# One normalising operation per four heads, with attention rows of 640 floats and their heads interleaved

## The chip, the core and the metric

The kernel runs on one core of one Trainium2 chip. A core has TensorE (PE; its weight loads are listed apart as PEld), VectorE (DVE), ScalarE (ACT), GpSimd (POOL) and SyncE (SP), which issues DMA transfers. The engines run side by side, each works through its own instructions in order, and they wait for one another with semaphores. The metric is the device time of one execution in microseconds (us); the median of the runs is compared.

## The reference

Attention over eight batches and eight heads of 576 queries, against keys and values pooled by eight to 72, followed by a mixture of experts: each token goes to the expert with the largest of eight logits, and its output is scaled by the gate's probability and by a second, sigmoid gate.

```python
k_p = k.reshape(B, H, Sp, pool, D).mean(axis=3)        # B=8, H=8, S=576, D=64, pool=8
v_p = v.reshape(B, H, Sp, pool, D).mean(axis=3)
attn = softmax(scale * q @ k_p.T)
x = (attn @ v_p).transpose(0, 2, 1, 3).reshape(B * S, H * D)      # 4608 x 512
logits = x @ w_gate                                    # 8 experts
e_idx = argmax(logits, axis=1)
eom = 1 / (1 + exp(-(x @ w_output_gate)))
for e in range(E):
    h = maximum(x[mask] @ w1[e], 0.0)                  # 512 -> 1024
    ye = h @ w2[e]                                     # 1024 -> 512
    out[mask] = gate_w[mask, None] * eom[mask, e, None] * ye
```

## The kernel before

**Attention and routing** work through 36 tiles of 128 tokens. Each tile has two halves (`a` is 0 or 1) of four heads, and a loop (L531 to L561) interleaves the steps of several tiles by hand. For half `a` of tile `i`:

- `scores` (L228): TensorE multiplies queries with the pooled keys; `peak` (L234): VectorE takes each head's maximum; `softmax` (L239): ScalarE exponentiates; `transpose_p` (L248, L249) turns the result two tiles later.
- `values` (L256): three tiles later TensorE multiplies the turned weights with `vbd`, the pooled values, into a PSUM tile `av`, of which there are two. Each head has COLS = 81 columns there: 64 outputs, 16 columns with that head's part of the two gates' logits, and the softmax's sum. L273 takes the sums' reciprocals on VectorE.
- `normalise` (L279, L281): VectorE multiplies the outputs by the reciprocals into `xg`, the tile's row of 512 floats in the order head, feature. A second operation does the same with the 4 x 16 logit parts, into a tile `graw` in the order head, logit.

For every group of four tiles `route` (L291 to L357) adds the eight heads' logit parts (L296), finds the expert and the token's place in that expert's list, and writes the gate's factor into the row. It is a chain of small VectorE operations that `work` spreads between the steps of the tiles. A row in `xg` has ROW = 514 floats: 512 features, the token's number (written by an `iota` on POOL, L268) and the factor (L344). POOL scatters each tile's rows to a table `xs` in device memory, by an indirect DMA per tile (L390), sorted by expert.

Beside this run the loading of keys, queries, values and the first weights (SP), the pooling of keys and values (POOL at L173, L174 and L188, VectorE at L191), and the splitting of the first weights in a high and a low part (L416 on ScalarE, L420 on VectorE).

**The change of stages.** `gather_early` (L395) waits for the rows of the first six groups and gathers the first three tiles of expert 0 into `xb` with three indirect DMAs. `turn_x` (L427 to L430) transposes each in four slices of 128 features, as the first layer wants them. Then the first layer's first job runs (L581) while `route` of the last group and `closing` (L361) compute the table of jobs on VectorE.

**The experts** take jobs of two or three tiles of 128 rows. For each, TensorE transposes the gathered rows (L830), multiplies with `w1` (L868) and with `w2` (L849); every factor is split in a high and a low part. ScalarE and VectorE move and split the results, VectorE applies the factor (L999), and POOL gathers the rows of a later job (L1085) and scatters the outputs (L1110). The weights of the even experts lie in `w1a` and `w2a`, those of the odd ones in `w1b` and `w2b`; SP loads pieces of them into six `stage` buffers.

**Memory.** The buffer `rows` holds `xb`, then the outputs `y_all`, then some scratch for the list of tiles (`past_rows` in the place of `y_all`, `line_rows` behind it). `w1b` and `w2b` are allocated behind `rows`.

## Time and profile before

| | |
|---|---|
| median of three runs | 664.21 us (663.7 to 667.07) |
| the profiled execution | 664.95 us, of which the span is 663.2 us |
| granted clock of TensorE, mean of the span | 0.98 |
| attention ends (last L281 starts) | at 180.0 us |
| first L849 of the experts' stage starts | at 199.68 us |
| DVE busy, of the span | 356.3 us (54%) |
| PE busy, of the span | 612.9 us (92%) |

All times inside the execution are counted from the start of the span. The shares of the span mix the two stages, so the stages have to be read apart. The profile names an instruction by its line, its engine, its operation, and the tiles that it writes and reads (`xg<-av,grec`); `x72` is how often it ran. A group's line gives the busy time of all and the mean of one. Two VectorE instructions in a row can overlap in the profile: the next one starts before the last one ends.

### The profile page before, as it was taken

Reading aid. Unit: us, or ns where it says so; the run is one execution under the profiler, and the core shown is the slowest. Engines: PE = TensorE matmul, PEld = TensorE weight load, DVE = VectorE, ACT = ScalarE, POOL = GpSimd, SP = SyncE. Lnnn points to the kernel's source line nnn. Section 1 sums busy time; section 2 is a strip of 40 time slices with the busy share of each in tenths; the row PEclk is TensorE's granted clock in tenths of the full one; section 3 lists DMA queues with packets and bytes.
Section 4 is the critical chain, followed back from the end, with each engine's and each line's share of the span. In section 5 each row is a group of like instructions: output and inputs, shape, how many; then the busy total and the mean of one; then the engine's idle time right before and its main releaser. Section 6 shows DMA issues by size and latency. Waiting matters only on the chain.

```text
span 663.2 us, 11977 instructions
## 1 busy us (share of the span) xinstructions
PE 612.9 (92%) x3715; PEld 558.4 (84%) x3716; DVE 356.3 (54%) x877; ACT 260.0 (39%) x693; POOL 217.4 (33%) x270
## 2 busy tenths in 40 slices
PE   0898988999978999999999999999998899999996
PEld 0787877988976999899798988999897898989895
DVE  5689989899883722577546422354142722222221
ACT  2776857888541511347244301333040420211110
POOL 3547628663432321231404112131222213030213
PEclk9998988999998899999989999999999899999999
DMA  8899757883435921467746422074113102020203
GB/s 268 275 290 285 225 181 263 251 231 121 129 144 177 315 80 49 122 215 248 272 139 209 149 70 61 19 231 134 55 22 134 32 20 80 16 63 32 64 32 77
DMA packets 28746, 95.82 MB, mean 144 GB/s; under 512 B 4735, under 2 KB 5759, under 8 KB 26882
## 3 DMA queue, kind: packets, MB, share of 16 engines
q1 hardware_dynamic: 18194, 61.92, 29.5%
q0 software_dynamic: 10480, 33.13, 15.1%
q8 instruction: 21, 0.34, 0.2%
q14 instruction: 51, 0.42, 0.2%
HBM read 76.13 MB, written 20.22 MB: 145 GB/s over the span
## 4 chain that ended last, share of the span: by engine, by line
PE 66%; issue 2%; DVE 1%; DVEq 0%; POOL 0%; ACT 0%; POOLq 0%
PE p_y L849 32%; PE p_h L868 31%; PE p_x L830 2%; DVE w1a L993 1%; PE p_y L830 0%; POOL out L1110 0%; DVE rows L999 0%; DVE xt L986 0%; ACT xt L933 0%; PE p_y L910 0%; DVE sums L1019 0%; DVEq L681 0%; DVEq L1018 0%; DVEq L1030 0%; DVEq L798 0%
## 5 line engine op out<-in xcount | busy, mean ns | idle before, releaser
L948 ACT ACTIVATE ht<-p_h 128x384 fp32r<-128x384 f32 (+1 forms) x104 | 46.8, 450 | 267.0 <-PE p_h L868 266.7
L868 PE MATMUL p_h<-xt,w1b 128*128 128x384 f32 (+1 forms) x736 | 117.8, 321 | 4.1 <-issue 3.0
L868 PEld LDWEIGHTS p_h<-xt,w1b 128*128 128x128 f32 x736 | 116.6, 191 | 5.4 <-issue 3.5
L849 PE MATMUL p_y<-w2a,ht 128*128 128x512 f32 x456 | 109.1, 399 | 6.2 <-issue 4.2
L1006 DVE SCALAR_TENSOR_TENSOR ht<-p_h,ht 128x384 fp32r<-128x384 f32 (+1 forms) x104 | 52.5, 505 | 114.9 <-ACT ht L948 114.8
L849 PE MATMUL p_y<-w2b,ht 128*128 128x512 f32 x480 | 113.6, 396 | 0.0
L849 PEld LDWEIGHTS p_y<-w2a,ht 128*128 128x128 f32 x456 | 87.1, 193 | 25.0 <-issue 6.7
L849 PEld LDWEIGHTS p_y<-w2b,ht 128*128 128x128 f32 x480 | 89.8, 188 | 20.5
L868 PE MATMUL p_h<-xt,w1a 128*128 128x256 f32 (+1 forms) x640 | 95.1, 309 | 4.2 <-DVE sums L1019 4.2
L868 PEld LDWEIGHTS p_h<-xt,w1a 128*128 128x128 f32 x640 | 94.4, 193 | 5.0 <-DVE sums L1019 4.4
L999 DVE TENSOR_SCALAR rows<-p_y,sc 128x512 f32<-128x512 f32 x41 | 30.5, 749 | 122.7 <-PE p_y L849 122.7
L1110 POOL DMA_INDIRECT out<-rows,dst x41 | 41.6, 1015 | 129.7 <-DVE rows L999 124.9
L256 PE MATMUL av<-vbd,pT 128*128 128x162 f32 (+1 forms) x480 | 75.6, 313 | 8.5 <-DVE vbd L216 2.9
L239 ACT ACTIVATE p<-p_h,m 128x72 f32<-128x72 f32 x288 | 70.9, 361 | 25.4 <-DVE m L234 25.2
L256 PEld LDWEIGHTS av<-vbd,pT 128*128 128x128 f32 (+1 forms) x480 | 62.8, 185 | 11.9 <-issue 6.4
L1085 POOL DMA_INDIRECT rows<-xs,src x51 | 58.6, 1149 | 24.2 <-POOL src L1081 13.9
L1080 POOL COPY nx<-rows 128x6 f32<-128x6 f32 x17 | 3.2, 190 | 149.1 <-PE p_y L830 71.2
L390 POOL DMA_INDIRECT xs<-xg,where x36 | 36.0, 1000 | 47.2 <-DVE where L345 22.9
L228 PE MATMUL p_h<-kbd,q_even 128*128 128x144 f32 (+1 forms) x160 | 30.6, 321 | 15.7 <-DMA q_even<-qT 12.2
L249 ACT ACTIVATE pT<-ptr 128x384 f32<-128x384 f32 x72 | 37.8, 526 | 5.7 <-PE ptr L248 5.6
L228 PEld LDWEIGHTS p_h<-kbd,q_even 128*128 128x128 f32 (+1 forms) x160 | 24.5, 203 | 17.1 <-issue 12.2
L248 PE MATMUL ptr<-ident,p 128*128 128x128 f32 x216 | 37.2, 283 | 1.8 <-DVE running L333 1.7
(172 smaller groups left out, 712.2 us busy)
## 6 DMA issues: line engine op xcount, KB each, us to landing
stage<-wst SPq DMA_DIRECT2D x64, 512.0 KB, 5.3
kq<-kT SPq DMA_DIRECT2D x7, 1152.0 KB
rows<-v SPq DMA_DIRECT2D x16, 288.0 KB
kq<-qT SPq DMA_DIRECT2D x4, 1152.0 KB
q_even<-qT SPq DMA_DIRECT2D x3, 1152.0 KB
rows<-v SPq DMA_DIRECT2D x8, 256.0 KB
rows<-v SPq DMA_DIRECT2D x8, 160.0 KB
kq<-kT SPq DMA_DIRECT2D x2, 576.0 KB
```

Of the source, the lines that this page charges most:

```text
L228: nc.tensor.matmul(s[r0:r0 + n, 144 * c:144 * c + 144], q_t[b][:, 2 * a + c, s0:s0 + n], kbd[b % 2][:, 2 * a + c, :], start=True, stop=True)
L239: nc.scalar.activation(pt[i % 3][:, 4 * a + h, 0:KEYS], sv[:, h], AF.Exp, bias=m[:, h:h + 1])
L248: nc.tensor.transpose(tr[:, P * c:P * c + P], src[:, o:o + P], ident)
L249: nc.scalar.activation(pT_t[i][:, 3 * a:3 * a + 3, :], tr[:, 0:384].rearrange("p (c n) -> p c n", c=3), AF.Copy)
L256: nc.tensor.matmul(av[r0:r0 + n, COLS * c:COLS * c + 2 * COLS], pT[:, 3 * a + c, r0:r0 + n], vbd[b % 2][:, a, c].rearrange("p h f -> p (h ...
L390: ins = nc.gpsimd.indirect_dma_start(out=xs, out_offset=bass.IndirectOffsetOnAxis(ap=where, axis=0), in_=x.bitcast(I32), in_offset=None)
L849: i = mm(p_y[k], ht[:, h, f, P * k:P * k + P], w[:, part, o:o + DM], start=(f == 0 and part == 0 and h == 0), stop=(f == 7 and h == 1))
L868: i = mm(to, w[:, part, o:o + P], x, start=(d == 0 and k == 0), stop=(d == 3 and k == len(terms) - 1))
L948: act(ht[:, 0, f, 0:size * P], p_h[f % 3][:, 0:size * P], AF.Relu).then_inc(q["hh"], 1)
L1006: nc.vector.scalar_tensor_tensor(ht[:, 1, f, 0:n], src, 0.0, ht[:, 0, f, 0:n].bitcast(F32), op0=ALU.max, op1=ALU.subtract).then_inc(q["hl" ...
L1085: nc.gpsimd.indirect_dma_start(out=xb[:, k].bitcast(I32), out_offset=None, in_=xs, in_offset=bass.IndirectOffsetOnAxis(ap=src[:, k:k + 1], ...
L1110: nc.gpsimd.indirect_dma_start(out=out, out_offset=bass.IndirectOffsetOnAxis(ap=dst[:, k:k + 1], axis=0), in_=yb[k], in_offset=None, bound ...
```

## The change

A row of `xg` gets 642 floats. Each half tile has HALF = 4 x (64 + 16) = 320 of them, in the order feature, head: the four heads' values of one feature lie side by side, and behind the 256 features follow the 64 logit parts in the same order (logit, head). The token's number and the factor are the last two floats (ID = 640).

`normalise` is one VectorE operation per half tile in place of two. It reads 80 columns of each head, in the order head, column, and writes `xg` with four floats between one column and the next. `graw` goes. `route` sums the logit parts straight out of `xg`, over the halves and the heads.

Everything that reads the rows follows: `features` gives the four slices of 128 features for the transposes; the rows of `w1` are brought into the same order on the host; the number and the factor are read at ID. The indirect DMAs move 642 floats per row. In `rows`, `line_rows` now lies in the space of `y_all`, behind `past_rows`; the buffer grows by 160 floats in each partition, and what is allocated behind it, `w1b` and `w2b` among it, moves by 640 bytes.

```diff
-ROW = DM + 2
+
+HALF = 4 * (D + 16)
+ID = 2 * HALF
+ROW = ID + 2
...
+def features(x, c):
+    o = HALF * (c // 2) + P * (c % 2)
+    return x[:, o:o + P]
...
-        nc.vector.memset(zrow[:, DM:DM + 1], float(N))
+        nc.vector.memset(zrow[:, ID:ID + 1], float(N))
...
-                graw[g] = p2.tile([P, GMAX, H, 16], F32, tag="graw", name=f"graw{g}")
...
-                nc.gpsimd.iota(xg[g][:, 0:n, DM], pattern=[[P, n]], base=t0 * P, channel_multiplier=1,
+                nc.gpsimd.iota(xg[g][:, 0:n, ID], pattern=[[P, n]], base=t0 * P, channel_multiplier=1,
...
-        nc.vector.tensor_tensor(xg[g][:, j, D * 4 * a:D * 4 * a + 4 * D].rearrange("p (h d) -> p h d", h=4), avv[:, :, 0:D],
-                                grec[g][:, j, hs].unsqueeze(2).to_broadcast([P, 4, D]), op=ALU.mult)
-        nc.vector.tensor_tensor(graw[g][:, j, hs], avv[:, :, D:D + 16], grec[g][:, j, hs].unsqueeze(2).to_broadcast([P, 4, 16]),
-                                op=ALU.mult)
+        nc.vector.tensor_tensor(xg[g][:, j, HALF * a:HALF * a + HALF].rearrange("p (f h) -> p h f", h=4), avv[:, :, 0:D + 16],
+                                grec[g][:, j, hs].unsqueeze(2).to_broadcast([P, 4, D + 16]), op=ALU.mult)
...
-        gw = graw[g][:, 0:n]
+        gw = xg[g][:, 0:n, 0:ID].rearrange("p j (a f h) -> p j f a h", a=2, h=4)[:, :, D:D + 16]
         lg = small(g, [P, n, 16], F32, "lg")
-        v_.tensor_reduce(lg, gw.rearrange("p j h f -> p j f h"), axis=AX.X, op=ALU.add)
+        v_.tensor_reduce(lg, gw, axis=AX.XY, op=ALU.add)
...
-        v_.reciprocal(xg[g][:, 0:n, DM + 1], rec)
+        v_.reciprocal(xg[g][:, 0:n, ID + 1], rec)
...
-            nc.tensor.transpose(tr[:, c], sh.xb[:, k, P * c:P * c + P], ident)
+            nc.tensor.transpose(tr[:, c], features(sh.xb[:, k], c), ident)
...
 def line_rows(sh, c0, c1):
-    o = WIDE * (ROW + DM) + 112
+    o = WIDE * ROW + 2 * (E - 1) * R
...
-                i = nc.tensor.transpose(p_x[k][:, c], xb[:, k, P * c:P * c + P], sh.ident)
+                i = nc.tensor.transpose(p_x[k][:, c], features(xb[:, k], c), sh.ident)
...
-            copy(nx, xb[:, :, DM:DM + 2]).then_inc(q["c"], 1)
+            copy(nx, xb[:, :, ID:ID + 2]).then_inc(q["c"], 1)
...
-        sh.rows = sb("rows", [P, WIDE * (ROW + DM) + 112 + 2 * R + 26], F32)
+        sh.rows = sb("rows", [P, WIDE * (ROW + DM) + 26], F32)
...
-            moe_w1.reshape(E, 4, P, FF).transpose(0, 2, 1, 3).reshape(E, P, 4096),
+            moe_w1.reshape(E, 2, 4, D, FF).transpose(0, 1, 3, 2, 4).reshape(E, 4, P, FF).transpose(0, 2, 1, 3).reshape(E, P, 4096),
```

More of the change, by code (lines that the diff above doesn't have):

```diff
@@ L218, in gate_v @@
                                     mask.unsqueeze(3).to_broadcast([P, 3, 2, 16]), op=ALU.mult)
-    s_t, pT_t, xg, graw, grec = {}, {}, {}, {}, {}
+    s_t, pT_t, xg, grec = {}, {}, {}, {}
     GMAX = max(GROUPS)
```

## The prediction

> **What bounds the kernel now.** I read the page first, then the busy time by stretches, the groups by line and form, the waits of TensorE, and the order of time in single stretches.
>
> ```profile
> PE 612.9 (92%) x3715; PEld 558.4 (84%) x3716; DVE 356.3 (54%) x877; ACT 260.0 (39%) x693; POOL 217.4 (33%) x270
> ```
>
> This is the page's line of busy time (engine, us, share, instructions). The stretches below give, after the bounds and the length, the busy time of PE, PEld, DVE, ACT and POOL, then PE's granted clock, the DMA share and GB/s:
>
> ```profile
> 40.00:60.00 20.00, 16.41 (x121) 14.51 (x120) 18.82 (x55) 13.04 (x51) 10.16 (x7) 0.91 0.98 295
> 60.00:80.00 20.00, 19.90 (x164) 18.82 (x164) 18.65 (x69) 16.14 (x63) 13.96 (x13) 1.00 0.76 235
> 80.00:100.00 20.00, 17.02 (x130) 15.54 (x130) 17.14 (x58) 13.24 (x51) 8.19 (x5) 0.91 0.59 216
> 100.00:120.00 20.00, 17.64 (x132) 15.94 (x131) 19.66 (x62) 13.99 (x53) 16.66 (x14) 0.91 0.77 257
> 120.00:140.00 20.00, 18.88 (x161) 17.47 (x159) 17.81 (x68) 15.67 (x60) 13.56 (x12) 1.00 0.82 256
> 140.00:160.00 20.00, 18.99 (x156) 17.46 (x153) 19.55 (x81) 17.92 (x70) 7.78 (x7) 1.00 0.49 148
> 160.00:180.00 20.00, 18.88 (x155) 17.63 (x154) 16.95 (x76) 14.34 (x48) 7.97 (x9) 1.00 0.39 140
> ...
> 340.00:380.00 40.00, 40.00 (x234) 37.15 (x233) 23.05 (x32) 17.35 (x28) 9.31 (x14) 1.00 0.60 194
> ```
>
> The page's 54% for DVE is an average over two stages with different limits. In the experts' stage TensorE alone sets the pace: from 340 to 380 us PE is busy 40.00 of 40.00. Attention, before it, has two engines near full: from 40 to 180 us the seven rows add up to 127.7 of 140 for PE and 128.6 for DVE. DVE has 11.4 us free there, PE 12.3. In four stretches of 20 us (40, 60, 100 and 140) DVE has only 1.18, 1.35, 0.34 and 0.45 us free. The next view, TensorE's waits in 40 to 184 us (total, times, longest), says who ends PE's idle time; its five longest:
>
> ```profile
> PE av L256 <- DVE vbd L216: 2.9, 1, 2.9
> PE av L256 <- DVE grec__3_1365 L339: 1.9, 1, 1.9
> PE ptr L248 <- DVE running L333: 1.7, 1, 1.7
> PE av L256 <- DVE graw L281: 1.6, 2, 1.1
> PE av L256 <- DVE zr L316: 1.5, 2, 1.1
> ```
>
> All name DVE: 9.6 us of PE's idle time. So work added to or taken from DVE in attention is felt in the span, though not one for one.
>
> **The change, part by part.** *One normalisation instead of two.* First the groups by form (us of all, mean ns of one), then a piece of DVE's order of time (start and length in us):
>
> ```profile
> L279 DVE TENSOR_TENSOR xg<-av,grec 128x256 f32<-128x256 f32 x72 | 30.3, 421 | 1.2
> ...
> L191 DVE TENSOR_REDUCE vp<-rows 128x64 f32<-128x256 f32 x42 | 23.9, 596 | 2.6 <-POOL rows L188 2.6
> ...
> L281 DVE TENSOR_TENSOR graw<-av,grec 128x64 f32<-128x64 f32 x72 | 15.3, 213 | 0.0
> ...
> L296 DVE TENSOR_REDUCE lg<-graw 128x64 f32<-128x512 f32 x9 | 9.2, 1024 | 0.0
> ...
> L191 DVE TENSOR_REDUCE vp<-rows 128x192 f32<-128x1536 f32 x2 | 5.5, 2756 | 4.9 <-DMA rows<-v 4.9
> ...
> L316 DVE TENSOR_REDUCE zr<-zs 128x4 f32<-128x32 f32 x9 | 1.6, 177 | 0.1
> ```
>
> ```profile
> 60.78 0.42 DVE L279 TENSOR_TENSOR xg<-av,grec 128x256 f32<-128x256 f32 x1
> 61.12 0.21 DVE L281 TENSOR_TENSOR graw<-av,grec 128x64 f32<-128x64 f32 x1
> 61.25 0.45 DVE L234 TENSOR_REDUCE m<-p_h 128x4 f32<-128x288 f32 x1
> ```
>
> The pair shows 421 + 213 ns, but successive operations overlap: start to start L279 takes 0.34 us and L281 0.13, so the pair holds DVE for 0.47 us. From 64 to 256 elements the time grows by 208 ns in 192, 1.083 ns an element. With dense writes the one operation of 320 elements would hold DVE for 0.34 + 64 x 1.083 ns = 0.41 us: 0.06 us saved, not the 0.21 of a whole operation.
>
> Its writes are not dense. The input runs through 80 adjacent floats of a head, and the output places them four floats apart, since the four heads are interleaved: each write lies 16 bytes behind the last. No row of this trace has a long strided write. The nearest rows are strided reads of SBUF: L191 sums values 64 floats apart, and between its two forms 1280 elements cost 2160 ns, 1.69 ns each, 0.60 above the dense rate. Bounds for the write: no excess (0.41 us), 0.60 as for the reads (0.41 + 320 x 0.60 ns = 0.60 us), or twice that (0.80 us). I take the middle, the only strided price that a row shows: +0.13 us x 72 = **+9.5 us of DVE**.
>
> The Trainium skill has this price ("Vector Engine (DVE) Microarchitecture Reference", 5.2 Measured stream behaviour on trn2): a port keeps its full rate only where elements come in runs of two or more adjacent 4-byte words, and the destination counts like the sources. The page gives 1.71 ns for a destination that hops at every element, about the reads' 1.69 above, and 2.50 for one that steps by 24 words; by the latter the operation would hold DVE some 0.86 us and the sum on DVE would be some +25 us, an estimate from that page. No row here shows a write.
>
> *The logits' sum.* L296 now reads floats 16 apart: 1024 ns for 512, the strided rate. Afterwards four neighbours lie together and the halves 320 floats apart. At the dense rate, from L316's 177 ns for 32 elements, it takes 177 + 480 x 1.083 = 697 ns: 0.33 x 9 = **-2.9 us**. If runs of four don't help, 0.
>
> DVE's net is +6.6 us, and the first row below (shortest, median and longest, first and last start) spreads the 72 calls over 154 us: 0.86 in each 20 us. In the four full stretches I let nine tenths through to PE (3.1), in the other three, with 2.2 to 3.1 us free, a third (0.9): **+4.0 us**. All of it would be 6.6, a third 2.2.
>
> ```profile
> L279 DVE TENSOR_TENSOR xg<-av,grec x72: 409/424/426, 26.0 to 179.7; 128x256 f32<-128x256 f32 x72
> ...
> L331 DVE TENSOR_SCALAR gden<-gden x9: 157/170/3989, 54.0 to 183.0; 128x4 f32<-128x4 f32 x9
> ```
>
> ```profile
> 106.09 3.58 POOL L188 TENSOR_TENSOR rows<-rows 128x768 f32<-128x768 f32 x2
> ...
> 105.72 3.99 DVE L331 TENSOR_SCALAR gden<-gden 128x4 f32<-128x4 f32 x1
> ```
>
> A second reason to expect less than all: small DVE operations are held up beside POOL's long ones. L331, 170 ns in the median, once took 3989 and ended with POOL's L188. DVE that comes later to such a place ends at the same moment; shifted, it can also meet or miss one. That is worth 3 us either way, and I keep it for the range.
>
> *Longer rows.* The 36 scatters and 54 gathers move 642 floats a row instead of 514, a quarter more. The DMA view (times, us to landing) and the order of time have:
>
> ```profile
> rows<-xs,src POOLq DMA_INDIRECT x54, 4.2
> ...
> xs<-xg,where POOLq DMA_INDIRECT x36, 4.9
> ```
>
> ```profile
> 169.08 1.12 POOL L400 DMA_INDIRECT rows<-xs,src  x1 [0.30 <-issue]
> ...
> 173.06 0.63 ACT L416 ACTIVATE w1a<-stage 128x512 fp32r<-128x512 f32 x1
> ...
> 174.54 0.63 PE L427 MATMUL xtr<-ident,rows 128*128 128x128 f32 x4 [1.12 <-ACT w1a L416]
> ...
> 199.98 1.05 POOL L1085 DMA_INDIRECT rows<-xs,src  x1 [0.83 <-POOL src L1081]
> ...
> 193.95 2.35 DVE L420 TENSOR_TENSOR w2a<-stage,w2a 128x1024 fp32r<-128x1024 f32 x2
> ```
>
> and from the chain that ended last:
>
> ```profile
> 212.33 0.45 PE p_x L830 x4
> ```
>
> One transfer counts: the second early gather (issued 169.08). PE waits 1.12 us for it until 174.54; ACT's L416, which the row names, ended at 173.69, so the gather is the likelier releaser. A row set of 263 KB at the 140 to 295 GB/s of the stretches above takes 0.9 to 1.9 us, 1.2 at some 220, so a quarter more is **+0.3 us**; bounds 0 and 1 (a quarter of a landing). In the experts' stage a gather has time: issued at 199.98, its first reader on PE is at 212.33, against 4.2 us to land. Without that cover the 17 later sets of three gathers would cost 0.3 each, 5 us. DMA issues on POOL and SP keep their number and order.
>
> *The end of attention.* DVE runs almost without a gap from the last normalisation to its last part of w2a (193.95, 2.35 us), so the last L296's -0.33 and the last normalisation's +0.13 act there directly: **-0.2 us**.
>
> *At nothing:* the weight rows' new order (same loads and matmuls); the transposes' slices, still 128 adjacent floats; the zero row's memset, 128 floats on one partition, in the start stretch. Moving w1b and w2b by 640 bytes:
>
> ```profile
> L868 PE MATMUL p_h<-xt,w1b 128*128 128x384 f32 x480 | 85.3, 338 | 0.0
> ...
> L868 PE MATMUL p_h<-xt,w1a 128*128 128x384 f32 x288 | 50.5, 334 | 0.0
> ```
>
> The two w1 buffers lie at different addresses and differ by 4 ns in 334, so I take 0 and keep 1 us either way.
>
> **Sum:** 4.0 + 0.3 - 0.2 = +4.1 us. The profiled execution took 664.95 us (span 663.2); with 4.1 it is 669.05. The median of the runs shown is 664.21, 0.74 below it, and 664.21 + 4.1 gives **668.3 us**.
>
> **The rivals.** *Writes at 16 bytes are free (the other side).* Place: the 72 calls; price: 0.41 us instead of 0.47, so -4.4 - 2.9 = -7.3 us on DVE. It decides if an excess of under 0.2 ns an element is paid (0.06 us over 320). About half passes, since only the 9.6 us of PE's waits on DVE can shrink and a held-up operation doesn't end sooner: -3.6, with +0.3 and -0.4 at the end -3.7: 660.5 us. [...] Against it: the reads' 1.69 ns. The Trainium skill ("SBUF — State Buffer", Door 1) says that SBUF lines have 16 bytes, and that fp32 can be strided by 4 for free, but also that two hits a line are needed; the second, with one hit a line here, speaks against it. No row here settles it.
>
> *Short hops cost double.* At 0.80 us the change adds 0.33 x 72 = 23.5, less 2.9: +20.6, of which 140/154, 18.7, between 40 and 180 us. DVE then has 128.6 + 18.7 = 147.3 us of work for 140. Of its 11.4 us free, 7.4 are waits for av, by its row in DVE's waits of 40 to 184 us; the other 4.0 lie between instructions and stay. 147.3 + 4.0 - 140 = +11.3, with +0.1 from the rest: 675.6 us. The 2.50 ns of the Trainium skill's page above would land here.
>
> ```profile
> DVE grec L273 <- PE av L256: 7.4, 11, 1.5
> ```
>
> *It is swallowed.* DVE's 11.4 us free take all of it, and only the +0.1 from transfer and end is left: 664.3 us. Against it: DVE ends PE's waits in every full stretch.
>
> **How the numbers follow.** A measurement of this kernel can tell about 0.5%, 3.3 us, from no change: under 660.9 is faster, over 667.5 slower. Forecast 0.62 (own range 665.5 to 671.5, from a third to all of 6.6 us), free writes 0.13, double 0.20, swallowed 0.05. Faster: half of the free writes and a little chance, 0.08. Same: the other half, the swallowed case and a quarter of the forecast, 0.28. Slower: 0.64. The range 664.0 to 676.5 leaves out the free writes and the top of the double case.
>
> **What would show it.** The one normalisation's mean: near 685 ns (421 + 64 x 1.083 + 320 x 0.60) for the forecast, 490 for free writes, near 880 for double. The logits' sum near 700 ns. DVE's busy time in attention up by about 6 us, PE's waits on DVE longer, and the experts' stage as long as before. I am wrong if the mean is 490, or if it is 685 and attention still ends where it did.

## The result and the profile after

| | before | after |
|---|---|---|
| median, same chip | 664.92 us (663.7 to 667.07, 4 runs) | 656.78 us (654.11 to 661.12, 4 runs) |
| ratio, 95% interval | | 0.9872 [0.983, 0.9914] |
| profiled execution (span) | 664.95 us (663.2) | 657.38 us (655.7) |
| granted clock of TensorE, mean | 0.980 | 0.987 |
| first L849 / L854 of the experts' stage | 199.68 us | 196.47 us |

The kernel became faster by 1.3%, where 668.3 us, slower by 0.6%, was forecast. One run of one kernel below (the changed kernel with the move taken back, 667.7 us) fell in a slower state of the chip and is left out of that kernel's figures. The lines of the new kernel lie 7 or 8 further down in attention (L279 is L286, L216 is L224) and 5 further in routing and experts' stage (L296 is L301, L849 is L854, L868 is L873).

First the groups by line and form of the kernel after (us of all, mean ns of one, idle time before), which answer to the rows of the prediction:

```profile
L286 DVE TENSOR_TENSOR xg<-av,grec 128x320 f32<-128x320 f32 x72 | 53.5, 743 | 1.2
...
L301 DVE TENSOR_REDUCE lg<-xg 128x64 f32<-128x512 f32 x9 | 6.0, 667 | 0.0
```

The one normalisation takes 743 ns (685 forecast), and start to start it holds VectorE for 0.584 us in the median (0.60 forecast; the pair before 0.472): 0.112 x 72 = 8.0 us more. The logits' sum fell by 357 ns x 9 = 3.2 us (2.9 forecast). VectorE has 4.8 us more to do, in place of the 6.6 forecast. So the price of the strided writes was read well; and yet the time fell.

Now TensorE's waits of 40 to 184 us in the kernel after (total, times, longest):

```profile
PE av L264 <- DVE xg L286: 2.4, 4, 1.2
PE av L264 <- DVE at L345: 2.1, 1, 2.1
PE av L264 <- DVE vbd L224: 1.6, 1, 1.6
PE xtr L432 <- POOL xg L275: 1.2, 1, 1.2
PE vtr L214 <- DVE vp L199: 1.0, 6, 0.2
```

VectorE still ends most of them. Its rows add up to 8.9 us, and to 10.4 in the same view of the kernel before, though it has more to do. Transfers are longer, as forecast, and the wait for the second early gather went from 1.12 to 1.2 us. The DMA view of the kernel after (times, us to landing; 4.2 and 4.9 before):

```profile
rows<-xs,src POOLq DMA_INDIRECT x54, 4.6
...
xs<-xg,where POOLq DMA_INDIRECT x36, 5.5
```

The stretches, with the columns explained in the prediction, of the kernel before:

```profile
40.00:80.00 40.00, 36.31 (x283) 33.33 (x282) 37.47 (x124) 29.18 (x112) 24.12 (x19) 0.96 0.87 265
80.00:97.00 17.00, 14.02 (x106) 12.54 (x106) 14.19 (x51) 10.24 (x39) 5.24 (x4) 0.90 0.53 207
97.00:170.00 73.00, 68.50 (x550) 63.08 (x549) 68.76 (x254) 59.76 (x226) 44.81 (x39) 0.98 0.65 206
```

and of the kernel after:

```profile
40.00:80.00 40.00, 36.02 (x289) 32.61 (x289) 38.41 (x109) 28.92 (x109) 23.66 (x18) 1.00 0.81 266
80.00:97.00 17.00, 16.83 (x142) 15.84 (x142) 15.77 (x54) 14.48 (x57) 9.50 (x8) 1.00 0.83 290
97.00:170.00 73.00, 66.43 (x534) 59.97 (x533) 69.20 (x220) 58.31 (x218) 43.89 (x41) 1.00 0.68 225
```

Read the counts in brackets: they say how much was done. To 80 us, and again from 97 to 170, both kernels do about the same. From 80 to 97 us TensorE does 142 matmuls after and 106 before: nearly all that attention gained lies in this one stretch.

The rest of the gain lies in the experts' stage. Here is the chain that ended last (start, us, what), first for the kernel before, then after:

```profile
222.94 16.67 PE p_h L868 x96
...
240.48 16.37 PE p_y L849 x72
...
457.79 16.79 PE p_y L849 x72
474.58 16.90 PE p_h L868 x96
```

```profile
236.82 16.37 PE p_y L854 x72
...
292.51 16.67 PE p_h L873 x96
...
455.05 16.36 PE p_y L854 x72
471.41 16.67 PE p_h L873 x96
```

The same 72 matmuls take 16.37 us early in the kernel before (weights `w2a`) and 16.79 late (`w2b`). Afterwards they take 16.35 to 16.38 everywhere. From start to start a 512-column matmul on `w2b` takes 232 ns before and 227 after, one of 384 columns on `w1b` 175 and 173; on `w2a` and `w1a` it was 227 and 173 all along. The groups by form, first of the kernel before (its `w1b` line is in the prediction), then after:

```profile
L849 PE MATMUL p_y<-w2b,ht 128*128 128x512 f32 x480 | 113.6, 396 | 0.0
```

```profile
L854 PE MATMUL p_y<-w2b,ht 128*128 128x512 f32 x480 | 111.1, 391 | 0.0
...
L873 PE MATMUL p_h<-xt,w1b 128*128 128x384 f32 x480 | 84.1, 334 | 0.0
```

`w2b` went from 113.6 to 111.1 us and `w1b` from 85.3 to 84.1: **3.7 us**, and what differs for these two buffers is the move of 640 bytes that the prediction put at nothing.

A third place is the expert with a single tile, near 510 us. TensorE's order of time before and after:

```profile
516.14 6.55 PE L868 MATMUL p_h<-xt,w1a 128*128 128x256 f32 x40 [4.20 <-DVE sums L1019]
```

```profile
510.59 6.54 PE L873 MATMUL p_h<-xt,w1a 128*128 128x256 f32 x40 [2.40 <-DVE sums L1024]
```

TensorE waits there for VectorE, which stands in "issue" itself (time in which the profile shows nothing that it waits for). The long pieces of it in the chain add up to 4.41 us before and 2.71 after:

```profile
509.51 2.75 issue
...
513.17 1.66 issue
```

```profile
505.75 0.48 issue
...
506.66 2.23 issue
```

The trace's records of instruction loads, 8192 bytes each, start at 510.5, 513.1, 515.2 and 515.5 us in the kernel before, and at 507.1, 509.5 and 511.2 after: four in this place, then three. VectorE's program has 72 instructions fewer (805 in place of 877), so its loops may lie elsewhere in these blocks.

Three candidates then: the moved buffers (about 3.7 us), the place of VectorE's code (about 2), and attention, where VectorE has more work and TensorE waits less.

### The profile page after: what moved, and what is told of

Read it like the earlier page. It is cut to its first block, busy times and chain, and to the rows that moved or that the text cites. A ratio compares the mean times of both kernels' runs of the same rounds, so it can differ in the third digit from the quotient of the medians.

```text
span 655.7 us, 11906 instructions
## 1 busy us (share of the span) xinstructions
PE 606.7 (93%) x3715; PEld 553.3 (84%) x3716; DVE 357.3 (54%) x805; ACT 260.0 (40%) x693; POOL 220.6 (34%) x270
## 4 chain that ended last, share of the span: by engine, by line
PE 64%; issue 2%; DVE 1%; DMA 1%; ACT 0%; DVEq 0%; POOL 0%; ACTq 0%; POOLq 0%
PE p_y L854 31%; PE p_h L873 31%; PE p_x L835 2%; DMA stage<-wst 1%; DVE w1a L998 1%; PE p_y L835 0%; DVE w1b L998 0%; DVE rows L1004 0%; ACT w2b L945 0%; POOL out L1115 0%; ACT w1b L945 0%; ACT xt L938 0%; DVE ht L1011 0%; DVEq L803 0%; PE p_y L915 0%
## 5 line engine op out<-in xcount | busy, mean ns | idle before, releaser
L873 PE MATMUL p_h<-xt,w1b 128*128 128x384 f32 (+1 forms) x736 | 117.0, 320 | 5.3 <-issue 5.3
L873 PEld LDWEIGHTS p_h<-xt,w1b 128*128 128x128 f32 x736 | 115.9, 192 | 6.6 <-issue 6.2
L854 PE MATMUL p_y<-w2a,ht 128*128 128x512 f32 x456 | 108.2, 397 | 5.9 <-issue 4.0
L854 PE MATMUL p_y<-w2b,ht 128*128 128x512 f32 x480 | 111.1, 391 | 0.0
L854 PEld LDWEIGHTS p_y<-w2a,ht 128*128 128x128 f32 x456 | 86.6, 192 | 24.4 <-issue 6.5
L854 PEld LDWEIGHTS p_y<-w2b,ht 128*128 128x128 f32 x480 | 89.5, 188 | 18.4
L873 PE MATMUL p_h<-xt,w1a 128*128 128x256 f32 (+1 forms) x640 | 95.4, 310 | 2.5 <-DVE sums L1024 2.4
L873 PEld LDWEIGHTS p_h<-xt,w1a 128*128 128x128 f32 x640 | 94.3, 193 | 3.5 <-DVE sums L1024 2.6
L286 DVE TENSOR_TENSOR xg<-av,grec 128x320 f32<-128x320 f32 x72 | 53.5, 743 | 1.2
L236 PE MATMUL p_h<-kbd,q_even 128*128 128x144 f32 (+1 forms) x160 | 29.3, 310 | 16.1 <-DMA q_even<-qT 12.6
L236 PEld LDWEIGHTS p_h<-kbd,q_even 128*128 128x128 f32 (+1 forms) x160 | 23.4, 195 | 17.5 <-issue 12.9
## 6 DMA issues: line engine op xcount, KB each, us to landing
stage<-wst SPq DMA_DIRECT2D x64, 512.0 KB, 5.4
```

The lines of the kernel that those rows point to most:

```text
L236: nc.tensor.matmul(s[r0:r0 + n, 144 * c:144 * c + 144], q_t[b][:, 2 * a + c, s0:s0 + n], kbd[b % 2][:, 2 * a + c, :], start=True, stop=True)
L286: nc.vector.tensor_tensor(xg[g][:, j, HALF * a:HALF * a + HALF].rearrange("p (f h) -> p h f", h=4), avv[:, :, 0:D + 16], grec[g][:, j, hs] ...
L854: i = mm(p_y[k], ht[:, h, f, P * k:P * k + P], w[:, part, o:o + DM], start=(f == 0 and part == 0 and h == 0), stop=(f == 7 and h == 1))
L873: i = mm(to, w[:, part, o:o + P], x, start=(d == 0 and k == 0), stop=(d == 3 and k == len(terms) - 1))
```

## The experiments

All runs of a group share a chip and its runs of the kernel before. These take 665.91 us (21 runs) for the three kernels of part 1 and the one dense operation; 666.37 (17) for the no-ops, the two strided operations and the first two placements of part 2; 666.03 (23) for the third placement, the two kernels with 72 memsets and the two dense operations; 666.56 (17) for the 128 memsets and the place put back; 666.04 (17) for part 5. Times are medians. The ratios to the kernel before, with their 95% interval, are those on record and differ by up to 0.3% from the quotients of the medians.

**1. The changed kernel again, the move alone, and the move taken back.**

> The changed kernel as it is, beside the others on one chip. Theory M (most of the gain comes from the new place of w1b and w2b, about 3.6 us in the experts' stage, and the rest, some 3 us, from attention) and theory N (the gain comes from the normalisation and the logits' sum alone) both expect about 657 us, 8 below the kernel before. A third theory, C (attention's 3 us are a matter of when the clock was granted low in the two profiled executions), expects about 661 us in the median, 4 below.

656.69 us (6 runs), 0.9845 [0.9803, 0.9887], as theories M and N expected. Theory C, with 661 us, falls.

The kernel before with `w1b` and `w2b` moved by 640 bytes and nothing else:

```diff
-        sh.rows = sb("rows", [P, WIDE * (ROW + DM) + 112 + 2 * R + 26], F32)
+        sh.rows = sb("rows", [P, WIDE * (ROW + DM) + 112 + 2 * R + 26 + 160], F32)
```

> The kernel before with w1b and w2b moved by 640 bytes and nothing else. Theory M: the matmuls that read w2b start every 227 ns instead of 233, those that read w1b every 173.6 instead of 176.0, the experts' stage is 3.6 us shorter, the time about 661.3 us, ratio 0.9945. Theory N: no change, 664.9 us.

662.12 us (10 runs), 0.9941 [0.9913, 0.9969]: 3.8 us less than before. `w2b` takes 111.1 us and `w1b` 84.1, as in the changed kernel.

The changed kernel with 96 floats more in `rows`, so that `w1b` and `w2b` lie at the same distance from a multiple of 256 bytes as before:

```diff
-        sh.rows = sb("rows", [P, WIDE * (ROW + DM) + 26], F32)
+        sh.rows = sb("rows", [P, WIDE * (ROW + DM) + 26 + 96], F32)
```

> The changed kernel with w1b and w2b 384 bytes further on, so that they lie 1024 bytes behind their place in the kernel before. Theory M (a matter of the address modulo 256, 512 or 1024 bytes): w2b's matmuls are back at 233 ns, the time is 3.6 us above the changed kernel's, about 660.4 us. Theory N: as the changed kernel, 656.8 us.

660.83 us (11 runs), 0.9912 [0.9882, 0.9943]: 4.1 us more than the changed kernel. `w2b` takes 113.6 us again. The move is worth 3.8 to 4.1 us from both sides; some 5 us of gain are left without it. So the theory of the move holds, with its price, and that of a gain from the normalisation alone falls.

**2. What about the address decides.** In the kernel before, the buffers `w1a`, `w2a`, `xt` and `ht` start 128 bytes behind a multiple of 256, `w1b` and `w2b` on one. First all of `w1b`, `w2b` by 256 bytes (64 floats more in `rows`); then everything behind `ident` by 128 bytes; then everything behind `w2a` by 128 bytes:

```diff
+        sb("ahead", [P, 32], F32)
         sh.xt = sb("xt", [P, 2, 4, WIDE * P], F32R)
```

> The kernel before with w1b and w2b moved by 256 bytes: their addresses stay at 0 by 256 bytes, and become 0 by 512. Theory A256 (the place within 256 bytes decides): the matmuls of 512 columns that read w2b still start 232 ns apart, and those of 384 columns that read w1b 175 ns: time as before, 664 to 666 us. Theory A512 (the place within 512 bytes decides): 227 and 173 ns, time about 662 us.

> The kernel before with every tile behind the identity moved by 128 bytes: w1a, w2a and the transposed operands come to 0 by 256 bytes, w1b and w2b to 128. Theory absolute (operands at 0 by 256 bytes are slow): w2b's matmuls start 227 ns apart, w2a's 232, so the loss changes sides and the time stays at 664 to 666 us. Theory relative (the two operands of a matmul in different halves of 256 bytes are slow): w2b stays at 232 ns and w2a at 227, unchanged. If neither is slow, the loss of 3.6 us is gone and the time is about 662 us; if both are, it is doubled, about 669 us.

> The kernel before with everything behind w2a moved by 128 bytes: xt and ht at 0 by 256 bytes, w1b and w2b at 128, w1a and w2a still at 128. Theory relative (a matmul is slow when its weights and its moving operand lie in different halves of 256 bytes): now all four are slow, w2a and w2b 232 ns from start to start, w1a and w1b 175 to 176: 3.6 us more than before, about 669 us. Theory of the pair (w1b and w2b are slow as such, whatever lies where): w2a 227 and w2b 232 as before, 664 to 667 us.

One execution each: 665.76, 668.08 and 671.57 us. The start-to-start times in ns:

```
                   place in 256 bytes             512 columns    384 columns
                   w?a    w?b    xt, ht           w2a    w2b     w1a    w1b
before             128      0    128              227    232     173    175
moved 640          128    128    128              227    227     173    173
moved 256          128      0    128              227    232     173    175
all moved 128        0    128      0              227    232     173    175
xt on moved 128    128    128      0              232    232     175    175
```

Within 256 bytes, not 512, is what counts, and the place of the two operands against each other: in the five placements run, a matmul is slow when its weights buffer and its other operand (`xt` or `ht`) start in different halves of 256 bytes. Only starts on a multiple of 256 and 128 behind one were run. Neither place by itself does it: `w2b` is fast at 128 when `ht` is at 128 too, and slow at 128 when `ht` is at 0. The groups by form of the last kernel show all four slow (before: 113.6, 109.1, 85.3, 50.5):

```profile
L849 PE MATMUL p_y<-w2b,ht 128*128 128x512 f32 x480 | 113.6, 396 | 0.0
L849 PE MATMUL p_y<-w2a,ht 128*128 128x512 f32 x456 | 110.7, 403 | 6.0 <-issue 4.1 <-DVE xt L986 2.0
L868 PE MATMUL p_h<-xt,w1b 128*128 128x384 f32 x480 | 85.3, 338 | 0.0
L868 PE MATMUL p_h<-xt,w1a 128*128 128x384 f32 x288 | 51.1, 338 | 0.0
```

**3. The place of VectorE's code.** The first attempt put 72 no-ops before VectorE's loops of the experts' stage. What is called the gap here is TensorE's wait for VectorE at the expert with a single tile: 4.20 us before, 2.40 after.

> The changed kernel with 72 VectorE no-ops put right in front of VectorE's loops of the experts, so that everything behind them stands at the place in VectorE's instruction stream that it had in the kernel before. Theory P (place in the stream): near 510 us the expert with a single tile makes VectorE stand still in 'issue' for 0.5 to 2.2 us longer when its instructions stand where they stood before, and TensorE's gap there goes back from 2.1-2.4 us to about 4.2 us: about 2 us more than the changed kernel, 658 to 659.5 us. Rival: the shorter gap comes from something else (clock, order of arrival); then the gap stays at 2.1-2.4 us and the time at 656 to 657.5 us. The no-ops themselves stand in a place where VectorE waits for the first sums of the experts; 72 of them should take less than 3 us there and may cost up to 1 us once, which the gap near 200 us would show.

656.2 us (6 runs), 0.986 [0.9819, 0.9902], gap 2.31 us. It decides nothing: the trace has 805 VectorE instructions as in the changed kernel and none of the no-ops, so nothing shows that the code moved. It serves as a repetition. Then 72 memsets, which the trace does show, once near the start and once at the door of the loops, right in front of them:

```diff
     ready_k(0)
+    for _ in range(72):
+        nc.vector.memset(sh.upto, 0.0)
     first_v(0)
```

```diff
+        for n in range(72):
+            nc.vector.memset(sums[:, n // 9, 8 * (n % 9):8 * (n % 9) + 8], 0.0)
         for f in range(F0, 8):
             eng.wait_ge(q["s2"], f - F0 + 1)
```

> The changed kernel with 72 VectorE memsets of 8 columns near its start, where VectorE stands idle from 6.8 to 11.5 us for the first values: all of VectorE's code behind them stands again where it stood in the kernel before and in the kernel with two normalising operations. Theory P (place of the code: VectorE stands still while 8 KB blocks of code are loaded, and how many loads fall on the expert with a single tile depends on the place): the gap of TensorE near 512 us is 4.2 us again instead of 2.1 to 2.4. If this is all, 658 to 660 us. Theory P+ (the place of the code is also what made the kernel with two operations 9.9 us slower than the changed one): 664 to 667 us. Rival (the second operation in each tile costs it, not the place): gap 2.1 to 2.4 us and 656 to 658 us.

> The changed kernel with 72 VectorE memsets at the door of the experts' loops: the attention's code stays where it is, the experts' code moves by 72 instructions. Theory P: the gap near 512 us is 4.2 us, and the experts' stage is 2 us longer; the memsets themselves take 4 to 5 us there, of which none to 3 us reach the end: 658 to 662 us. Rival (no effect of the place): gap 2.1 to 2.4 us, 656.5 to 660 us.

Near the start: 670.88 us (6 runs), 1.0102 [1.0057, 1.0146]. The memsets took 9.5 us there, twice the pause that they were to fill, and TensorE's wait for the first keys grew from 3.5 to 11.0 us, so the time says nothing of the place; the gap does: 4.19 us, at 522.9 us. At the door: 660.35 us (10 runs), 0.9933 [0.9901, 0.9965], and TensorE's order of time has:

```profile
515.10 6.54 PE L873 MATMUL p_h<-xt,w1a 128*128 128x256 f32 x40 [4.19 <-DVE sums L1024]
```

The same with 128 memsets, as many instructions as the theory gives to a block:

> The changed kernel with 128 VectorE memsets (8 KB of code, one block as the trace shows its code loads) at the door of the experts' loops. Theory P by blocks: the loops stand at the same place within a block as in the changed kernel, so three loads and not four fall on the expert with a single tile and the gap near 512 us is 2.1 to 2.4 us again (4.19 us with 72 memsets). The memsets cost what 128 of them take there, below 3 us: 656.5 to 659.5 us. Rival (more code in all, or the memsets themselves, lengthen the gap): 4.2 us or more, 660 to 663 us.

659.21 us (4 runs), 0.9876 [0.9822, 0.993]:

```profile
514.17 5.06 PE L873 MATMUL p_h<-xt,w1a 128*128 128x256 f32 x40 [2.31 <-DVE sums L1024]
```

72 instructions lengthen the gap by 2 us, 128 do not, and neither do 72 + 56 in the kernel with the place put back below (2.10 us). The instruction loads agree: four in this place with 72 memsets (509.5, 512.0, 514.1, 514.5 us), three with 128 (510.5, 513.1, 515.0). So a shift by 128 instructions leaves the gap as it was, and one by 72 does not: the place of the loops within such a block decides, and it is worth 2 us of this gap. The whole times are less sharp: 659.21 and 660.35 us don't part within their intervals, and in both the memsets run too.

**4. One operation or two, dense or strided.** Two kernels part the normalisation again, into 64 and 16 columns per head, with the new layout of the rows; one walks the output densely (feature, head) and lets the reads from PSUM jump; one does that with two operations.

```diff
-        nc.vector.tensor_tensor(xg[g][:, j, HALF * a:HALF * a + HALF].rearrange("p (f h) -> p h f", h=4), avv[:, :, 0:D + 16],
-                                grec[g][:, j, hs].unsqueeze(2).to_broadcast([P, 4, D + 16]), op=ALU.mult)
+        nc.vector.tensor_tensor(xg[g][:, j, HALF * a:HALF * a + HALF].rearrange("p (f h) -> p f h", h=4),
+                                avv[:, :, 0:D + 16].rearrange("p h f -> p f h"),
+                                grec[g][:, j, hs].unsqueeze(1).to_broadcast([P, D + 16, 4]), op=ALU.mult)
```

The dense operation:

> The changed kernel with the normalisation run in the order feature, head: it writes adjacent floats and reads PSUM 81 floats apart. If the excess of 743 ns over a dense 490 is the strided write's, and strided PSUM reads are free, the operation takes 490 ns and VectorE is spared 18 us. If attention's time follows VectorE's work, a third to a half of that passes, 6 to 9 us: about 649 us. If it doesn't follow VectorE, about 656.8 us. If strided PSUM reads cost as much, the operation stays near 740 ns.

Two strided operations:

```diff
+        o = xg[g][:, j, HALF * a:HALF * a + HALF].rearrange("p (f h) -> p h f", h=4)
+        for f0, f1 in ((0, D), (D, D + 16)):
+            nc.vector.tensor_tensor(o[:, :, f0:f1], avv[:, :, f0:f1],
+                                    grec[g][:, j, hs].unsqueeze(2).to_broadcast([P, 4, f1 - f0]), op=ALU.mult)
```

> The changed kernel with the normalisation done again by two operations (64 and 16 columns per head) that write the same rows of 640 floats: 72 VectorE instructions more, the same bytes at the same addresses. Theory 'VectorE passes a quarter': the pair takes 0.71 us to the next start instead of 0.58 (0.13 us more, 9.4 us of VectorE in all), of which 2.2 us reach the end; with the place in the stream (2 us) 660 to 661.5 us. Theory 'VectorE passes two thirds' (as forecast): 6 us and 2 us, 664 to 665 us. If VectorE's own work is hidden altogether: 658 to 659 us by the place in the stream alone, or 657 without it.

Two dense operations, parted at the same columns:

> The version that walks the output rows densely, with two operations for one (64 and 16 columns of each head): 72 instructions more and about 0.05 us more per pair, 3.7 us of VectorE, than the dense version (653.8 us). Theory P: the gap near 510 us grows by 2 us, and a quarter of VectorE's 3.7 us comes on top: 656 to 657.5 us. Theory 'a second operation per tile costs 7 us or more whatever its length': 661 to 665 us. If neither counts: 654 to 655 us.

The two strided operations once more, with 56 memsets at the door of the loops, which puts the loops back at the changed kernel's place within a block:

> The kernel with two normalising operations and 56 VectorE memsets at the door of the experts' loops, 128 instructions more than the changed kernel in all. Theory P by blocks: the gap near 515 us is 2.1 to 2.4 us (4.25 us without the memsets), and the time falls from 666.6 us by 2 to 4 us, to 662.5 to 665 us; what is left to the changed kernel's 656.5 us, 6 to 8 us, then is the second operation in each tile. If the place were all, 656.5 to 658 us. If it were nothing, 666.5 to 668 us.

| | VectorE per half tile, start to start | median | ratio |
|---|---|---|---|
| one, strided (the change, again) | 0.581 us (0.584 in the first profile) | 656.69 us (6) | 0.9845 [0.9803, 0.9887] |
| two, strided | 0.463 + 0.120 = 0.583 us | 666.62 us (12) | 1.0012 [0.9988, 1.0037] |
| two, strided, place put back | as above | 664.69 us (12) | 0.9972 [0.9949, 0.9996] |
| one, dense | 0.408 us | 653.8 us (6) | 0.9793 [0.9751, 0.9834] |
| two, dense | 0.341 + 0.131 = 0.472 us | 662.41 us (12) | 0.9953 [0.9923, 0.9983] |

The groups by form of the kernels with two strided operations and with one dense:

```profile
L288 DVE TENSOR_TENSOR xg<-av,grec 128x256 f32<-128x256 f32 x72 | 44.9, 624 | 1.2
L288 DVE TENSOR_TENSOR xg<-av,grec 128x64 f32<-128x64 f32 x72 | 20.1, 280 | 0.0
```

```profile
L286 DVE TENSOR_TENSOR xg<-av,grec 128x320 f32<-128x320 f32 x72 | 35.1, 488 | 1.2
```

Two strided operations hold VectorE just as long as one, where 0.71 us were expected, and yet the kernel is 9.9 us slower. Two dense operations cost 8.6 us more than one, as the theory of a cost whatever the length expected, where 2.2 to 3.7 would have been place and VectorE's time. With the place put back the gap is 2.10 us and the time falls by 1.9 us; **8 us stay with the second operation itself**, though VectorE's time is the same. (Against the changed kernel with 128 memsets, which ran on the same chip and has its loops at the same place, 659.21 us in only 4 runs, it is 5.5 us.)

Where are they? Starts in us of the 25th, 31st, 67th and 72nd reciprocal of attention (one for each half tile), and of the first second-layer matmul of the experts:

```
                         25th   31st   67th   72nd   experts
before                   79.9   96.8  170.5  179.4    199.7
before, moved 640        79.8   97.2  171.0  179.0    199.3
two, strided             80.0   97.1  171.3  182.9    203.0
two, place put back      80.4   98.6  173.1  183.1    203.3
the change               80.4   93.0  167.1  176.5    196.5
the change again         79.3   95.0  169.0  178.6    198.6
change, move taken back  80.4   98.2  172.3  181.2    201.2
change, no-ops           79.5   92.1  166.3  175.7    195.7
two, dense               78.1   94.0  167.0  176.2    196.5
one, dense               80.2   92.3  164.9  174.1    194.2
```

To the 25th and from the 31st to the 67th the strided kernels keep the same pace, with one operation or two. The stretch between takes 12.1 to 18.2 us, and the time from the 67th to the experts 28.3 to 31.7. Single executions differ in that stretch even with the same operations (12.6, 15.7 and 17.8 with the change's), so it has more than one way to go. By the first second-layer matmul the two kernels with two strided operations are at 203.0 and 203.3 us, the four with one at 195.7 to 201.2, 198.0 in the mean: some 5 of the 8 us lie ahead of it. About one of them is TensorE's wait before it transposes the early gather's rows, between 167 and 176 us: 2.1 and 2.0 us with two strided operations and 0.7 to 1.2 in the four with one.

What the ways are, the 19 kept profiles show, when TensorE's longest gap in this stretch is set beside the clock records:

```
                                     profiles   length of the stretch
no gap over 0.8 us                      4        12.1 to 12.6 us
gap of 1.2 to 2.8 us, clock full        5        14.0 to 15.9 us
gap of 2.5 to 3.6 us, half speed
  for 3.41 or 6.83 us at its end       10        16.8 to 18.3 us
```

All four of the first row have one operation. Of the nine with two, eight are in the last row and one in the middle; of the ten with one, two are in the last row.

**5. A hold-up beside GpSimd.** In that stretch a short VectorE operation of the routing, 0.19 us in the kernel after, stood for 3.31 us in the kernel before, about until GpSimd's two additions of pooled values ended; behind it waited the value operand `vbd`, and for that TensorE. The order of time of the kernel before (start, length), for VectorE, for GpSimd and for TensorE:

```profile
81.42 3.31 DVE L310 TENSOR_TENSOR oh<-cand,best 128x32 bf16<-128x32 f32 x1
...
85.44 0.41 DVE L216 TENSOR_TENSOR vbd<-vg,mask 128x96 f32<-128x96 f32 x2
```

```profile
81.11 3.57 POOL L188 TENSOR_TENSOR rows<-rows 128x768 f32<-128x768 f32 x2
```

```profile
85.74 1.04 PE L256 MATMUL av<-vbd,pT 128*64 128x162 f32 x10 [2.91 <-DVE vbd L216]
```

and of the kernel after, for VectorE and GpSimd, whose additions start behind the short operation:

```profile
81.97 0.19 DVE L315 TENSOR_TENSOR oh<-cand,best 128x32 bf16<-128x32 f32 x1
...
82.97 0.41 DVE L224 TENSOR_TENSOR vbd<-vg,mask 128x96 f32<-128x96 f32 x2
```

```profile
82.42 3.60 POOL L196 TENSOR_TENSOR rows<-rows 128x768 f32<-128x768 f32 x2 [0.82 <-issue]
```

The Trainium skill ("SBUF — State Buffer", Who interferes with whom) has one contention on the engines' side of SBUF, an exclusive lock on a port pair that VectorE and GpSimd share; the 3.31 us that end with the additions agree. TensorE's gap at this place is 2.81 to 3.60 us in the five profiled kernels with the old operations and in both with two strided ones, 1.2 to 1.7 us in three others, 2.69 in the kernel with memsets near the start, and there is none in the profiles of the change, of its repetition with the no-ops and of one dense operation. But two other profiled executions with the change's own attention have it (2.81 and 3.5 us). To test it, the second addition was put half a tile later:

```diff
         at(f - 2.5, halve_v, b)
+        at(f - 2, halve_v1, b)
```

> The kernel before with GpSimd's two additions of a sequence's values parted: the second half a tile later. Theory H (hold-up: a short VectorE operation that meets the pair of additions stands through both, 3.3 us, and TensorE stands 2.9 to 3.6 us for the value operand behind it): no hold-up near 81 us over 1.9 us, TensorE's gap near 86 us 1.8 us or less, the stretch from the 25th to the 31st normalised half tile 13 to 15.5 us (16.9 to 18.3 us before), and 662.5 to 664.5 us (before 666). Rival (the stretch is long for another reason): 17 us and more there, 665.5 to 667 us.

> The changed kernel with the same parting of the additions. Theory H: the stretch is 12.5 to 14.5 us in every run, and where runs of the changed kernel met the hold-up by chance they no longer do: 654.5 to 656.5 us (changed 656.5 us). Rival: 656 to 657.5 us.

> The dense version with the same parting. Its stretch is 12.1 us already, so theory H expects little: 652.5 to 654.5 us (dense 653.8 us). Rival (parting the additions costs GpSimd's scatters a place in the queue): 655 us or more.

In this order: 666.86 us (12 runs), 1.0001 [0.9974, 1.0027]; 655.48 us (6), 0.9837 [0.9789, 0.9885]; 652.15 us (6), 0.9781 [0.9744, 0.9819]. It did not part what it should: in the kernel before, the additions still followed each other at this place without a break (81.58 and 83.34 us), and now two operations were held up one after the other. In the profile of the changed kernel two were held up as well (1.53 and 1.72 us), and its stretch took 16.9 us where 12.5 to 14.5 were expected, so its median inside the expected range says nothing for theory H. VectorE's order of time in the kernel before with the parting:

```profile
81.94 1.49 DVE L312 TENSOR_TENSOR oh<-cand,best 128x32 bf16<-128x32 f32 x1
...
83.47 1.72 DVE L316 TENSOR_TENSOR zs<-lg,oh 128x32 f32<-128x32 f32 x1
```

So the hold-up is seen, but that it is the cause of the 8 us is not shown. The last kernel, 2.2% under the kernel before, has the lowest median of all; its interval overlaps that of the dense kernel without the parting, and both medians lie below every other.

**6. The clock.** TensorE's granted clock, over all runs of a kernel, splits the time in a part lost to the clock, (1 - mean clock) x time, and the rest:

| | mean clock | lost | rest |
|---|---|---|---|
| before (21 runs) | 0.9810 | 12.7 us | 653.3 us |
| before, moved 640 (10) | 0.9816 | 12.2 us | 650.2 us |
| two, strided (12) | 0.9804 | 13.1 us | 653.7 us |
| two, place put back (12) | 0.9807 | 12.9 us | 651.9 us |
| two, dense (12) | 0.9799 | 13.3 us | 649.1 us |
| the change again (6) | 0.9892 | 7.1 us | 649.4 us |
| the change, no-ops (6) | 0.9872 | 8.4 us | 648.4 us |
| the change, move taken back (11) | 0.9849 | 10.0 us | 651.1 us |
| the change, 72 memsets at the door (10) | 0.9850 | 9.9 us | 650.6 us |
| the change, 128 memsets (4) | 0.9868 | 8.7 us | 649.9 us |
| the change, 72 memsets near the start (6) | 0.9823 | 11.9 us | 659.5 us |
| one, dense (6) | 0.9885 | 7.5 us | 645.8 us |

All kernels with two operations lose 12 to 13 us, those with one 7 to 10, and 11.9 with the memsets near the start. Between the two strided operations and the changed kernel, as run again and with the no-ops, it is 6.0 and 4.7 us: by this account 4 to 6 us of the difference are half-speed windows that TensorE no longer meets. The account ties them to the second operation; it doesn't say how. The rest column shows the move (3.1 us) and the place (1.8 us) as gains of their own.

## Why the prediction was wrong

- **Strided writes, logits' sum, longer rows: right.** 743 ns for 685, 667 for 697, net VectorE +4.8 us for +6.6. Free writes and doubled hops are both ruled out. Of the two figures of the Trainium skill ("Vector Engine (DVE) Microarchitecture Reference", 5.2 Measured stream behaviour on trn2) the 1.71 ns fits better than the 2.50: (743 - 488) / 320 = 0.80 ns above the dense rate of 1.083, 1.88 in all.
- **What of VectorE's work reaches the end: right in size, as far as the intervals tell.** From the kernel before with the move (662.1) to the two strided operations (666.6) the operations' number and the code's place stay, and VectorE's net is (0.583 - 0.472) x 72 - 3.2 = +4.8 us, with the longer rows beside it: +4.5 us in time, some 2.5 either way, where the prediction had 4.0 + 0.3 - 0.2 = 4.1. Its working let three fifths of 6.6 us through; here nearly all of 4.8 passed, so that the totals agree is in part luck.
- **"Moving w1b and w2b by 640 bytes": the step that failed first.** It was put at 0, at most 1 us, from 338 and 334 ns in the groups. Times 480 that difference alone is 1.9 us, and the `w2b` group of the same view was not looked at. The chain of the kernel before had 16.79 and 16.37 us for the same 72 matmuls. It measured -3.8 us. The prediction's own sign, the experts' stage as long as before, failed with it: from its first second-layer matmul to the end of the span it took 463.5 us before and 459.2 after.
- **"One normalisation instead of two": the second.** The step counted VectorE's time from start to start and nothing else. Taking the second operation out is worth -9.9 us at equal VectorE time: -1.9 by the place of the code, which no step had, and -8 (-5.5 in the comparison on one chip) that are measured but explained only in part (4 to 6 us by the clock, with the slow stretch of 80 to 97 us and attention's end as the places where it shows). The prediction had seen that short operations are held up beside GpSimd's additions, but counted it as 3 us either way, for the range alone.
- **The rivals.** Swallowed, free writes and double hops were all about VectorE's time; none had the mechanism that decided.

Summed along the kernels that were run: -3.8 (move), +4.5 (VectorE's net and longer rows), -9.9 (one operation, place included) = -9.2 us, which is the first repetition's distance, 665.91 - 656.69 (the kernels ran on two chips, whose times of the kernel before differ by 0.5 us). The sum must close, since each kernel is compared with the next; the parts are what was measured. Open is why a second operation of 0.12 us that adds nothing to VectorE's time makes TensorE meet longer gaps and more half-speed windows.

## What to carry to other kernels

When a buffer moves, look up where the operands of each hot matmul start within 256 bytes, and compare the same group of matmuls on either buffer in the chain: 0.42 us in 16.4 was visible before the change. When instructions come or go on an engine whose loops branch, the loops' code moves too; look for "issue" in the chain and for instruction loads beside it. An operation taken out of an interleaved schedule can be worth far more or less than its own time, so try it in both orders (here: dense or strided, one or two) before a price is put on it.

## What the runs showed of the hardware that was not expected

- Two matmul operands of which one starts on a multiple of 256 bytes and the other 128 behind one cost 5 ns on 227 (512 columns) and 2 on 173 (384 columns).
- A VectorE operation that writes four floats apart takes 743 ns for 320 elements; the same elements with dense writes and strided PSUM reads take 488. The order of the walk is free to choose, and here the side in PSUM is the one to stride.
- VectorE stood for 1.66 to 2.75 us at a time in "issue" beside records of instruction loads of 8192 bytes, and 72 instructions more or less moved TensorE's gap by 2 us.
- After pauses of TensorE the clock records show half speed in pieces of 3.41 us or twice that. The same pause of 1.95 us near 215 us had a piece beside it in some profiled executions and none in others, one of 3.9 us or more nearly always. The Trainium skill ("TensorE: Matmul & The Clock Gate", What's actually happening) has a free-running window of 3413 ns; the lengths agree.
